# New durations in a list scheduler's model: an attention kernel with two feed-forward layers

## The chip, the cores and the metric

The kernel runs on one core of one Trainium2 chip. A core has five engines that each work through their own instructions in order: TensorE (PE, matrix products), VectorE (DVE), ScalarE (ACT), GpSimd (POOL) and SyncE (SP, which here issues all DMAs). They wait for one another by semaphores. The metric is device time in microseconds (us) of the whole kernel, the median of several runs; lower is better.

## The reference

```python
def _attn_ref(q, k, v, f):                     # (4, 8, 576, 64), f: (4, 8, 576)
    scores = scale * np.matmul(q, k.transpose(0, 1, 3, 2))
    cum = np.cumsum(np.log(np.clip(f, 0.0001, 1.0)), axis=-1)
    scores = np.where(causal, -1e9, scores + cum[..., :, None] - cum[..., None, :])
    return softmax(scores) @ v
def _moe_ref(x, w_in, w_out):                  # x: (2304, 512), w_in: (512, 2048)
    h = x @ w_in
    return np.maximum(0.01 * h, h) @ w_out
def _moe2_ref(x, w_in, w_out, g_ln):           # w_in: (512, 1024)
    h = x @ w_in
    solu = h * softmax(h)
    return (layer_norm(solu) * g_ln) @ w_out
```

The three run one after the other: causal attention with decay (4 batches, 8 heads, 576 positions), a feed-forward layer (FFN) on 2304 tokens with a hidden width of 2048, and a second layer with a width of 1024, whose activation is followed by a normalization.

## The kernel before

**Work and tiles.** Every fp32 product is made of three fp32r products of split operands: each operand is stored as a high part and the rest (`copy_f` makes the high part, `sub_f` the rest). Attention works on 16 pairs of heads (4 pairs for each batch). Of a pair, `prep_split` loads and splits q and k (`raw` to `kq`), `prep_v` scales and splits v, `scores` and `scores4` make the masked scores in PSUM tiles `ps_s`, `softmax` does maximum, exp (L647), sum, reciprocal and the split into f16 (`hl`), a DMA transposes `hl` to `pt`, `pv` multiplies by v into `ps_v`, and `evac` writes `xr` (L729 on ACT, L732 on DVE), which is spilled to DRAM as `xs_d`. The first four pairs are done in two passes, `(0, 1)` and `(2, 3, 4)` of their row blocks.

The FFN works on nine blocks of 256 tokens and 16 chunks of 128 hidden columns. `ffn_a` does chunks 0 to 8 (`FA`) while attention is still running, as far as batches are done: `load_x` brings x back as `xw` and splits it into `x`, `hidden` makes `ps_f<-x,wi` and its leaky ReLU `g` (L843 and L844 on ACT, L845 on DVE), and the output product is `ps_f<-g,wo`. Block 2 is the first that needs batch 1, block 4 the first that needs batch 2, block 6 the first that needs batch 3. When attention is finished, its SBUF and PSUM are handed to phase 2: `ffn_b` does chunks 9 to 15 (`wib`, `wob`) and `layer2` the second layer (`ph`, the normalization, a transposition through `tr`, and the output product). The weights are loaded and split by `weight` (`wst` or `raw`, an upper part `wk`, then the two parts).

**What sets the order.** Nothing above is emitted in the order in which it is written. `P.op` records each step as an `Op` with its engine (or several, for `flex` steps such as `copy_f` and `sub_f`), a duration in ns, a priority and the buffers that it writes and reads. `Plan.run` then walks through time: whenever an engine is free in its model, the ready step with the lowest priority number is emitted on it, a `flex` step only if `better_elsewhere` finds no engine on which it would end earlier. So the modelled durations decide two things: the order of each engine's instructions, and which engine does a `flex` step. On the chip each engine then runs its list in order and waits by semaphores. The model of before has three kinds of durations:

```python
def dve(n):                              # VectorE, n columns; act() and pool1() are alike
    return 1.042 * n + 70
def mmr(n):                              # a matmul of n columns
    return n / 2.4 + 2.5 if n > 255 else 80.0
```

a rule for the matmul clock, `pe_time`, which doubles a matmul's duration while PE was not busy enough in the windows before, and a single DMA queue with a rate (`nbytes / 360.0`).

## Time and profile before

| | us |
|---|---|
| median of 3 runs | 852.63 (852.53 to 854.60) |
| the profiled execution | 854.78 |
| its span, first to last instruction | 852.9 |
| PE busy | 787.6 |
| DVE, ACT, POOL busy | 495.8, 477.6, 338.6 |

A row of the profile that names `ps_f<-x,wi` is the instruction that writes tile ps_f and reads x and wi. Busy time is the union of an engine's instructions. An engine's idle time costs something only when the work behind it sets the end. L numbers are lines of the kernel of before; a helper's line stands for all that call it (L474 is every matmul, L428, L431 and L435 are `copy_f` on ACT, DVE and POOL, L443 is `sub_f`).

### The profile page before, as it was taken

How to read it: one execution, taken by the hardware profiler on the slowest of the kernel's cores; microseconds unless marked ns; L12 is line 12 of the kernel's file. 1: busy time of each engine (PE TensorE's matmuls, PEld its weight loads, DVE VectorE, ACT ScalarE, POOL GpSimd, SP SyncE). 2: the span in 40 equal slices, each digit the busy share in tenths (PEclk: the TensorE clock that was granted, in tenths of full speed). 3: DMA queues.
4: the chain of work that ended last, by engine and by line, in shares of the span. 5: the costliest groups of instructions: out<-in, count | busy, mean ns of one | idle time of the engine just before them, and what ended most of it. 6: DMA issues, size and time to landing. Idle time of an engine off the chain costs nothing.

```text
span 852.9 us, 15613 instructions
## 1 busy us (share of the span) xinstructions
PE 787.6 (92%) x5648; PEld 707.1 (83%) x5648; DVE 495.8 (58%) x1269; ACT 477.6 (56%) x1208; POOL 338.6 (40%) x402
## 2 busy tenths in 40 slices
PE   2567899997699999999999999999999999999997
PEld 2334599986699999999999988898889988998985
DVE  4787688787778768735544756334442444243641
ACT  3878788888888988845645533332333243324321
POOL 5566555474655484025121324321332133213321
PEclk9999989996799999999999999999999999999999
DMA  7899878899968997646555514231314131312113
GB/s 211 200 276 245 209 155 190 171 202 213 224 152 192 188 216 168 154 124 208 171 166 172 179 32 99 47 89 26 87 38 100 25 87 38 88 25 62 25 41 95
DMA packets 181958, 114.95 MB, mean 135 GB/s; under 512 B 147030, under 2 KB 163054, under 8 KB 181850
## 3 DMA queue, kind: packets, MB, share of 16 engines
q1 hardware_dynamic: 181882, 113.97, 55.5%
q8 instruction: 44, 0.72, 0.4%
q14 instruction: 32, 0.26, 0.1%
HBM read 64.32 MB, written 15.16 MB: 93 GB/s over the span
## 4 chain that ended last, share of the span: by engine, by line
PE 66%; ACT 7%; DMA 6%; DVE 5%; issue 3%; POOL 2%; SPq 0%; ACTq 0%; DVEq 0%; POOLq 0%
PE ps_f L474 41%; PE ph L474 11%; PE py L474 8%; PE ps_s L474 4%; PE ps_v L474 3%; DMA pt<-hl 3%; ACT hl L428 1%; ACT ps_s L647 1%; DMA xw<-xs_d 1%; DVE hl L439 1%; DMA tr<-hl 1%; ACT kq L428 1%; DMA raw<-wa 1%; ACT xr L729 1%; ACT g L843 1%
## 5 line engine op out<-in xcount | busy, mean ns | idle before, releaser
L474 PE MATMUL ps_f<-x,wi 128*128 128x256 f32 x972 | 131.4, 290 | 2.1 <-DVE g L845 2.1
L474 PEld LDWEIGHTS ps_f<-x,wi 128*128 128x128 f32 x972 | 124.9, 195 | 3.3 <-DVE g L845 2.9
L474 PE MATMUL ps_f<-g,wo 128*128 128x256 f32 x972 | 124.1, 283 | 0.0
L474 PEld LDWEIGHTS ps_f<-g,wo 128*128 128x128 f32 x972 | 119.3, 189 | 0.6 <-DVE g L845 0.2
L474 PE MATMUL ps_f<-x,wib 128*128 128x256 f32 x756 | 98.4, 281 | 0.7 <-DVE g L845 0.4
L474 PE MATMUL ph<-wi,g 128*128 128x512 f32 x408 | 98.3, 397 | 0.0
L843 ACT ACTIVATE g<-ps_f 128x256 fp32r<-128x256 f32 x144 | 55.1, 383 | 72.8 <-PE ps_f L474 70.9
L474 PEld LDWEIGHTS ps_f<-x,wib 128*128 128x128 f32 x756 | 92.8, 189 | 1.8 <-DVE g L845 1.7
L439 DVE SCALAR_TENSOR_TENSOR hl<-ps_s,st,hl 128x512 f16<-128x512 f32 (+4 forms) x160 | 82.4, 540 | 18.6 <-ACT hl L428 17.5
L474 PEld LDWEIGHTS ph<-wi,g 128*128 128x128 f32 x408 | 76.1, 189 | 17.5
L443 POOL TENSOR_TENSOR kq<-raw,kq 64x576 fp32r<-64x576 f32 (+2 forms) x49 | 74.0, 1510 | 36.6 <-ACT kq L428 34.2
L647 ACT ACTIVATE ps_s<-ps_s,st 128x512 f32<-128x512 f32 (+4 forms) x160 | 78.9, 493 | 15.7 <-DVE st L697 7.6
L474 PEld LDWEIGHTS <-VT 128*128 128x128 f16 x928 | 55.2, 108 | 37.2 <-issue 20.3
L474 PE MATMUL ps_f<-wo,x 128*128 128x512 f32 x348 | 84.0, 397 | 0.0
L845 DVE TENSOR_TENSOR g<-ps_f,g 128x256 fp32r<-128x256 f32 x144 | 60.3, 420 | 39.4 <-ACT ps_f L844 38.6
L474 PE MATMUL ps_v<-pt,VT 128*128 128x128 f16 (+1 forms) x928 | 63.2, 230 | 18.6 <-DVE xr L732 9.6
L474 PE MATMUL ps_s<-kq 128*128 128x512 f32 (+9 forms) x304 | 73.7, 365 | 6.8 <-DVE hl L439 6.7
L428 ACT ACTIVATE hl<-ps_s,st 128x512 f16<-128x512 f32 (+4 forms) x152 | 74.7, 529 | 9.1 <-DVE st L665 4.2
L474 PEld LDWEIGHTS ps_f<-wo,x 128*128 128x128 f32 x348 | 64.7, 189 | 15.1 <-ACT x L428 0.4
L474 PE MATMUL py<-g,wob 128*128 128x256 f32 x567 | 76.7, 280 | 0.0
L474 PEld LDWEIGHTS py<-g,wob 128*128 128x128 f32 x567 | 72.4, 188 | 1.9
L697 DVE CUSTOM_DVE_ANT_0 ps_s<-ps_s,mask 128x128 f32<-128x128 f32 (+3 forms) x128 | 62.3, 497 | 19.3 <-PE ps_s L474 17.1
(148 smaller groups left out, 1180.0 us busy)
## 6 DMA issues: line engine op xcount, KB each, us to landing
raw<-kq SPq DMA_DIRECT2D x24, 608.0 KB
wst<-wa SPq DMA_DIRECT2D x17, 512.0 KB
raw<-wa SPq DMA_DIRECT2D x15, 512.0 KB
xw<-xs_d SPq DMA_DIRECT2D x24, 256.0 KB
yp_d<-yo SPq DMA_DIRECT2D x36, 128.0 KB
yw<-yp_d SPq DMA_DIRECT2D x18, 256.0 KB
out<-ot SPq DMA_DIRECT2D x18, 256.0 KB
vr<-vt SPq DMA_DIRECT2D x13, 320.0 KB
```

What stands on the lines that cost most here:

```text
L428: nc.scalar.activation(o, i, CP, scale=1.0 if scale is None else scale)
L439: nc.vector.scalar_tensor_tensor(o, a, scale, b, op0=ALU.mult, op1=ALU.subtract)
L443: (nc.vector if eng == DVE else nc.gpsimd).tensor_tensor(o, a, b, op=ALU.subtract)
L474: nc.tensor.matmul(o, lhsT=l, rhs=r, start=start, stop=stop)
L647: P.op(ACT, act(W, 1, True) + 93, lambda view=view, j=j, k=k: nc.scalar.activation(view(), view(), AF.Exp, bias=sts.t[:, j:j + 1], scale=- ...
L697: P.op(DVE, dve(W) + 130, lambda i=i, j=j, view=view: nc.vector.tensor_tensor_reduce(view(), view(), mask[:, 384 - 128 * i:512], -0.125, 3 ...
L729: P.op(ACT, act(n, 1, True), lambda: nc.scalar.activation(xr.t[a:a + 64, dst0:dst0 + n], ps.t[b:b + 64, c0:c1], CP, scale=u.t[b:b + 64]), ...
L843: P.op(ACT, act(n, 0, True), lambda: nc.scalar.activation(g.t[:, 0, 0:n], h(), AF.Prelu, scale=WSC, alpha=0.01), eprio, w=[(g, 0)], r=[ps])
L845: P.op(DVE, dve(n) + 60, lambda: nc.vector.tensor_tensor(g.t[:, 1, 0:n], h(), g.t[:, 0, 0:n].bitcast(F32), op=ALU.subtract), eprio, w=[(g, ...
```

## The change

The change replaces numbers and one rule of the planner's model. `act`, `pool1`, `pool2`, `mmr`, `mmh` and the fixed parts of DVE steps become the durations of this kernel's own trace; a matmul of 256 columns goes from 109 to 119 ns, for instance. DMAs become slower in the model (`nbytes / 320.0`; a transposition takes 1.6 ns for each column of its source in the DMA queue and not 0.875). The clock rule `pe_time` is dropped. A new flag `port` marks DVE steps whose operands all lie in SBUF; `beside` stretches such a step to 1/0.58 of its length as long as the model has POOL busy. The steps themselves, buffers, priorities, weights and all other constants stay.

```diff
+LOCK = 0.58
...
-        def pe_time(d, t, heat):
...
+        def beside(d, t):
+
+            r = max(free_at["POOL"] - t, 0.0)
+            return d / LOCK if d <= LOCK * r else r + d - LOCK * r
...
                     hold = o.dur
-                    if e == "PE":
-                        hold = pe_time(hold, now, o.heat)
+                    if e == "DVE" and o.port:
+                        hold = beside(hold, now)
...
+def dvep(n):
+    return 1.05 * n + 125
...
 def act(n, extra=0, psum=False):
-    return 0.833 * n + (52 if psum else 95) + 93 * extra
+    return 0.83 * n + (150 if psum else 125) + 118 * extra
...
 def mmr(n):
-    return n / 2.4 + 2.5 if n > 255 else 80.0
+    return n * 0.4545 + 3.0 if n > 255 else 116.0
...
     def copy_f(o, i, n, prio, engs=(ACT, DVE, POOL), scale=None, psum=False, **kw):
         p = 0 if scale is None else 1
-        d = {ACT: act(n, p, psum), DVE: (dve(n) if psum else dve2(n)) + 60 * p, POOL: pool1(n) + 84 * p}
+        d = {ACT: act(n, 0, psum), DVE: dvep(n) if psum else dve2(n) + 30 * p, POOL: pool1(n) + 84 * p}
...
-        return flex(engs, [d[e] for e in engs], lambda e: queue[e].dma_start(dst(), src()), prio, dma=nbytes / 360.0, **kw)
+        return flex(engs, [d[e] for e in engs], lambda e: queue[e].dma_start(dst(), src()), prio, dma=nbytes / 320.0, **kw)
...
-        return P.op(SP, max(350.0 + 0.875 * n, 1175.0), lambda: nc.sync.dma_start_transpose(out=dst(), in_=src()), prio, dma=0.875 * n, **kw)
+        return P.op(SP, max(350.0 + 0.875 * n, 1175.0), lambda: nc.sync.dma_start_transpose(out=dst(), in_=src()), prio, dma=1.6 * n, **kw)
```

What comes of it in the order of the instructions, at three places.

On ACT, at the head of the program, where the first weights are split and the first softmax begins; before:

```order
L428 ACTIVATE wi_64<-wst_151 128x512
L428 ACTIVATE wk_83<-wst_152 128x512
L647 ACTIVATE ps_s_163,st_120<-ps_s_163,st_120 128x128
L609 ACTIVATE VT_106,va_136<-vr_105 128x640
L647 ACTIVATE ps_s_163,st_120<-ps_s_163,st_120 128x256
L609 ACTIVATE VT_107,va_137<-vre_156 128x640
```

and after (the lines stand 13 lower in the changed kernel, so L647 is L634):

```order
L415 ACTIVATE wi_64<-wst_151 128x512
L634 ACTIVATE ps_s_163,st_120<-ps_s_163,st_120 128x128
L634 ACTIVATE ps_s_163,st_120<-ps_s_163,st_120 128x256
L634 ACTIVATE ps_s_164,st_121<-ps_s_164,st_121 128x128
L646 ACTIVATE st_120<-st_120 128x2
L634 ACTIVATE ps_s_165,st_122<-ps_s_165,st_122 128x128
```

The weight copy to wk_83 has moved to POOL, and the sums over v (L609) stand behind more exps.

On PE, where FFN block 2 begins (the first row with x and wi) among the scores of a pair; before:

```order
L474 MATMUL ps_s_163<-kq_0_143 128x64
L474 MATMUL ps_s_163<-kq_1_144 128x64
L474 MATMUL ps_f_157<-x_810,wi_63 128x256 x3
L474 MATMUL ps_f_157<-x_811,wi_63 128x256 x3
L474 MATMUL ps_f_157<-x_812,wi_63 128x256 x3
L474 MATMUL ps_f_157<-x_813,wi_63 128x256 x3
```

and after:

```order
L461 MATMUL ps_v_167<-pt_132,VT_106 128x128
L461 MATMUL ps_s_166<-kq_0_143 128x128
L461 MATMUL ps_s_166<-kq_1_144 128x128
L461 MATMUL ps_f_158<-x_782,wi_63 128x256 x3
L461 MATMUL ps_f_158<-x_783,wi_63 128x256 x3
L461 MATMUL ps_f_158<-x_784,wi_63 128x256 x3
L461 MATMUL ps_f_158<-x_785,wi_63 128x256 x3
```

A further group of PV products (20 matmuls into ps_v) and four score products now stand ahead of block 2.

On PE, behind the last PV product of attention; before:

```order
L474 MATMUL ps_v_167<-pt_131,VT_109 128x128
L474 MATMUL ps_f_158<-g_824,wo_78 128x256 x3
L474 MATMUL ps_f_158<-g_825,wo_79 128x256 x3
L474 MATMUL ps_f_158<-g_826,wo_80 128x256 x3
L474 MATMUL ps_f_158<-g_827,wo_72 128x256 x3
```

and after:

```order
L461 MATMUL ps_v_167<-pt_131,VT_109 128x128
L461 MATMUL ps_f_158<-x_786,wi_69 128x256 x3
L461 MATMUL ps_f_158<-x_787,wi_69 128x256 x3
L461 MATMUL ps_f_158<-x_788,wi_69 128x256 x3
L461 MATMUL ps_f_158<-x_789,wi_69 128x256 x3
```

Attention now ends while block 5 is still in its hidden product; three more chunks of it and the whole of its output product follow.

## Rows read from the trace of the kernel before

**Rows 1.** The page: busy time of the engines, PE and its clock in 40 slices

```profile
PE 787.6 (92%) x5648; PEld 707.1 (83%) x5648; DVE 495.8 (58%) x1269; ACT 477.6 (56%) x1208; POOL 338.6 (40%) x402
...
PE   2567899997699999999999999999999999999997
...
PEclk9999989996799999999999999999999999999999
```

**Rows 2.** Busy time (instructions) by stretch, us: PE, PEld, DVE, ACT, POOL, clock, DMA

```profile
0.00:100.00 100.00, 62.54 (x240) 37.61 (x241) 69.45 (x200) 67.87 (x163) 59.42 (x68) 1.00 0.90 230
100.00:180.00 80.00, 75.24 (x675) 70.80 (x674) 64.99 (x202) 67.32 (x192) 43.91 (x44) 0.96 0.81 175
180.00:240.00 60.00, 46.03 (x345) 41.45 (x344) 45.38 (x150) 50.40 (x138) 37.66 (x37) 0.77 0.93 213
240.00:365.00 125.00, 123.74 (x1202) 119.99 (x1201) 95.77 (x316) 108.13 (x310) 58.10 (x61) 1.00 0.83 176
365.00:416.00 51.00, 49.53 (x421) 49.07 (x420) 22.62 (x37) 24.35 (x61) 18.79 (x22) 1.00 0.60 182
416.00:814.00 398.00, 397.08 (x2638) 362.41 (x2637) 184.10 (x350) 150.53 (x334) 112.98 (x160) 1.00 0.31 79
814.00:853.00 39.00, 33.44 (x141) 25.74 (x139) 13.51 (x20) 8.97 (x15) 7.75 (x13) 0.98 0.24 61
```

**Rows 3.** Timeline of the head: start, length in us, instruction, idle time before it

```profile
17.46 0.14 DVE L697 DVE_READ_ACCUMULATOR2_ANT st<- 128x1 f32 x1
...
18.66 0.78 ACT L428 ACTIVATE wk<-wst 128x512 f16<-128x512 bf16 x1 [6.82 <-DMA wst<-wa]
19.31 0.31 ACT L647 ACTIVATE ps_s<-ps_s,st 128x128 f32<-128x128 f32 x1
```

**Rows 4.** Groups by line and shape on ACT: count, busy us, mean ns, idle before

```profile
L428 ACT ACTIVATE kq<-raw 128x1216 fp32r<-128x1216 f32 x12 | 14.6, 1217 | 2.5 <-DMA raw<-kq 1.3 <-PE ps_s L474 1.2
...
L428 ACT ACTIVATE x<-xw 128x256 fp32r<-128x256 f32 x39 | 14.4, 411 | 4.5 <-DMA xw<-xs_d 4.3
...
L428 ACT ACTIVATE kq<-kq 64x640 fp32r<-64x640 f32 x12 | 8.8, 731 | 0.1
...
L428 ACT ACTIVATE VT<-vre,vs 128x640 f16<-128x640 f32 x2 | 1.6, 811 | 0.0
```

**Rows 5.** Timeline around the start of FFN block 2

```profile
213.92 0.33 SPq L465 DMA_DIRECT2D xs_d<-xr  x1
...
218.56 2.11 SPq L465 DMA_DIRECT2D xw<-xs_d  x4
...
223.95 3.00 PE L474 MATMUL ps_f<-x,wi 128*128 128x256 f32 x12
```

**Rows 6.** Pieces of the chain that ended last: start, us, what

```profile
209.97 2.16 PE ps_v L474 x20
...
352.53 0.36 PE ps_s L474 x4
...
354.40 1.13 PE ps_v L474 x20
...
416.78 52.51 PE ps_f L474 x432
```

**Rows 7.** Timeline: a DVE and a POOL instruction side by side

```profile
110.00 1.54 POOL L443 TENSOR_TENSOR kq<-raw,kq 64x640 fp32r<-64x640 f32 x1
110.05 2.11 DVE L443 TENSOR_TENSOR kq<-raw,kq 64x576 fp32r<-64x576 f32 x1
```

**Rows 8.** DVE's longest waits from 240 to 365 us: total, times, longest

```profile
DVE ps_s L697 <- PE ps_s L474: 6.8, 9, 1.5
DVE hl L439 <- ACT hl L428: 6.3, 13, 1.1
```

**Rows 9.** Timeline of phase 2: a block's last output products, splits of y, ph

```profile
487.08 0.52 PE L474 MATMUL ps_f<-g,wob 128*128 128x256 f32 x3
...
489.41 2.02 POOL L443 TENSOR_TENSOR g<-yo,g 128x256 fp32r<-128x256 f32 x2
...
491.69 3.67 PE L474 MATMUL ph<-wi,g 128*128 128x512 f32 x15
```

More of the change, by code (lines that the diff above doesn't have):

```diff
@@ L92 @@
 class Op:
-    __slots__ = ("eng", "dur", "emit", "bufs", "prio", "npred", "succ", "seq", "taken", "dma", "weight", "heat")
+    __slots__ = ("eng", "dur", "emit", "bufs", "prio", "npred", "succ", "seq", "taken", "dma", "weight", "heat", "port")
 WEIGHT = {"DVE": 4.25}
@@ L171, in run @@
         left = len(self.ops)
-        warm, win, busy = False, 0, 0.0
         def push(t, kind, x):
@@ L218, in bequeath @@
                     self.tags[nm].free.append(view)
-        def pe_time(d, t, heat):
-            nonlocal warm, win, busy
-            k = int(t // WINDOW)
-            while win < k:
-                u = busy / WINDOW
-                warm = u > 0.8 or (warm and u > 0.38)
-                busy, win = 0.0, win + 1
-            end = t
-            while d > 1e-6:
-                edge = (win + 1) * WINDOW
-                f = 1.0 if warm else 2.0
-                step = min(d * f, edge - end)
-                d -= step / f
-                end += step
-                busy += step * heat
-                if end >= edge - 1e-6:
-                    u = busy / WINDOW
-                    warm = u > 0.8 or (warm and u > 0.38)
-                    busy, win = 0.0, win + 1
-            return end - t
+        def beside(d, t):
+            r = max(free_at["POOL"] - t, 0.0)
+            return d / LOCK if d <= LOCK * r else r + d - LOCK * r
         for o in self.ops:
@@ L453, in copy_f, with sub_f @@
         p = 0 if scale is None else 1
-        d = {ACT: act(n, p, psum), DVE: (dve(n) if psum else dve2(n)) + 60 * p, POOL: pool1(n) + 84 * p}
-        return flex(engs, [d[e] for e in engs], lambda e: copy_on(e, o(), i(), scale and scale()), prio, **kw)
-    def sub_f(o, a, b, n, prio, engs=(DVE, POOL), scale=None, **kw):
-        d = {DVE: dve(n) + (60 if scale else 0), POOL: pool2(n) + (pool1(n) + 40 if scale else 0)}
-        return flex(engs, [d[e] for e in engs], lambda e: sub_on(e, o(), a(), b(), scale and scale()), prio, **kw)
+        d = {ACT: act(n, 0, psum), DVE: dvep(n) if psum else dve2(n) + 30 * p, POOL: pool1(n) + 84 * p}
+        return flex(engs, [d[e] for e in engs], lambda e: copy_on(e, o(), i(), scale and scale()), prio, port=not psum, **kw)
+    def sub_f(o, a, b, n, prio, engs=(DVE, POOL), scale=None, psum=False, **kw):
+        d = {DVE: dvep(n) if psum else dve(n) + (60 if scale else 0), POOL: pool2(n) + (pool1(n) + 40 if scale else 0)}
+        return flex(engs, [d[e] for e in engs], lambda e: sub_on(e, o(), a(), b(), scale and scale()), prio, port=not psum, **kw)
     queue = {SP: nc.sync, ACT: nc.scalar, POOL: nc.gpsimd}
@@ L672, in softmax @@
                 sub_f(lambda lo=lo, w=w: hl.t[:, lo:lo + w], lambda so=so, w=w, view=view: view()[:, so:so + w],
-                      lambda ho=ho, w=w: hl.t[:, ho:ho + w], w, prio, engs=(DVE,), scale=rs,
+                      lambda ho=ho, w=w: hl.t[:, ho:ho + w], w, prio, engs=(DVE,), scale=rs, psum=True,
                       w=[(hl, lo)], r=[ps, (sts, 4), (hl, ho)])
@@ L731, in evac @@
             w=[(xr, (hd, dst0))], r=[ps, u])
-        P.op(DVE, dve(n) + 60, lambda: nc.vector.scalar_tensor_tensor(
+        P.op(DVE, 0.97 * n + 240, lambda: nc.vector.scalar_tensor_tensor(
             xr.t[a:a + 64, dst0:dst0 + n], ps.t[a:a + 64, c0:c1], u.t[a:a + 64],
@@ L801, in weight @@
         copy_f(up, top, 512, prio, engs=T_ENGS, scale=lambda: 0.5, w=[k], r=[s])
-        P.op(DVE, dve(512), lambda: nc.vector.scalar_tensor_tensor(
-            low(), low(), 13, k.t, op0=ALU.logical_shift_right, op1=ALU.bitwise_or), prio, rw=[s], r=[k])
+        P.op(DVE, dve(512) + 40, lambda: nc.vector.scalar_tensor_tensor(
+            low(), low(), 13, k.t, op0=ALU.logical_shift_right, op1=ALU.bitwise_or), prio, rw=[s], r=[k], port=True)
         copy_f(lambda: dst.t[:, 0], kf, 512, prio, scale=scale, w=[(dst, 0)], r=[s])
@@ L843, in hidden @@
         P.op(ACT, act(n, 0, True), lambda: nc.scalar.activation(g.t[:, 0, 0:n], h(), AF.Prelu, scale=WSC, alpha=0.01), eprio, w=[(g, 0)], r=[ps])
-        P.op(ACT, act(n, 0, True), lambda: nc.scalar.activation(h(), h(), AF.Prelu, scale=WSC, alpha=0.01), eprio, rw=[ps])
-        P.op(DVE, dve(n) + 60, lambda: nc.vector.tensor_tensor(
+        P.op(ACT, act(n, 0, True) - 90, lambda: nc.scalar.activation(h(), h(), AF.Prelu, scale=WSC, alpha=0.01), eprio, rw=[ps])
+        P.op(DVE, dve(n) + 10, lambda: nc.vector.tensor_tensor(
             g.t[:, 1, 0:n], h(), g.t[:, 0, 0:n].bitcast(F32), op=ALU.subtract), eprio, w=[(g, 1)], r=[ps, (g, 0)])
```

18 lines of the change are left out of this document (9 added, 9 removed).

## The prediction

> **What bounds the kernel now.** I read the page first, then the busy time of the engines in seven stretches, then the waits and the timeline of the stretches in which TensorE (PE) stands idle. The page says that PE is busy for 92% of the span, far more than the others, and its row of slices shows where it is not: in the first quarter, in two slices near 200 us, and in the last slice [rows 1]. The stretches put numbers on it [rows 2]. From 416 to 814 us PE is busy for 397.08 of 398 us: there the FFN runs with hardly a gap and no order can gain anything. From 240 to 365 us it is busy for 123.74 of 125. What is idle lies elsewhere: 37.5 us before 100 us, 4.8 us from 100 to 180, 14.0 us from 180 to 240, 1.5 us around the switch from attention to FFN (365 to 416), and 5.6 us in the tail after 814. In the stretch from 180 to 240 the granted clock is also only 0.77, so the matmuls there run in part at the lower level: twenty attention matmuls took 2.16 us at 210 us and 1.13 us at 354 us [rows 6].
>
> So the end is "the time at which PE becomes full" plus "the PE work left at that time" plus small change. PE becomes full when FFN block 2 can start. That block needs the attention of all eight heads of batch 1, its spill to DRAM, the reload and the split of x; until then PE has only scores and PV, and the chain of exp, reciprocal, copy and transpose sets the pace. In that time ScalarE (ACT) is the fullest of the other engines: 67.32 of 80 us and then 50.40 of 60 us [rows 2], against 64.99 and 45.38 for VectorE (DVE). The spill of the last head pair of batch 1 is issued at 213.92 us, x comes back by DMA issues at 218.56, and the matmuls of block 2 run from 223.95 us on [rows 5].
>
> **The change part by part.** It removes and adds no arithmetic. It changes the numbers that the planner believes, so each engine gets another order, and the instructions that may run on several engines are dealt out otherwise. PE has 5648 matmuls before and after. I went through both orders and priced what stands ahead of the same place in each by the mean durations of before.
>
> *The head.* Before, ACT's eighth row is a weight copy (wk from wst_152) that waits 6.82 us for its load; the first exp stands behind it and starts at 19.31 us, though the row maximum it needs is read out by 17.60 us (17.46 + 0.14) [rows 3]. After, the copy is on GpSimd (POOL) and the exp comes directly after the two weight splits, at 17.6 us if nothing else holds it: 1.7 us earlier. Bounds: 0, if the loads set the pace anyway (the DMA share of the first 100 us is 0.90 [rows 2]), and 1.7. I take 1.7, since ACT carries the whole softmax that follows: **-1.7 us**.
>
> *ACT and DVE up to block 2.* Up to the first evacuation of block 2, ACT has 360 rows instead of 366: five copies kq to kq fewer at 731 ns (-3.7), five x copies fewer at 411 ns (-2.1), but two raw to kq more at 1217 ns (+2.4), three V scalings more at 811 ns (+2.4) [rows 4], and a few smaller ones, among them a further piece of softmax: in sum +0.8 us. DVE has 13 rows more there, +2.7 us in sum. Both do that extra work for attention that has moved ahead of block 2 (next part). Since ACT is the fuller one, I take **+0.8 us**, and 2.7 us as the bound if DVE sets the time.
>
> *PE up to block 2.* Before, 502 PV matmuls and 192 score matmuls stand ahead of block 2; after, 522 and 196. Twenty PV matmuls cost 1.13 us at full clock and four score matmuls 0.36 us [rows 6]. They run in time that is idle and are then missing from the full stretch: **-1.5 us**, with bounds 0 and -2.5 (their price at the low clock).
>
> *Attention against FFN up to 373 us.* After, 1152 of the 1944 matmuls of the first FFN half stand ahead of the last PV, before 1200. These 48, at 52.51 us for 432 [rows 6], are 5.8 us of FFN that moves behind attention. Up to ACT's last evacuation its work falls by 5.9 us: seven kq to kq copies fewer (-5.1), three x copies fewer (-1.2), three FFN evacuation pairs fewer (-2.3), against three V scalings (+2.4) and others [rows 4]. So attention can end some 5 us earlier, and the FFN that is left is as much more: no gain by itself. But where block 6 needs the last batch, its first matmul now has 15.3 us of other matmuls behind the last PV instead of 11.4. PE's idle time there is 1.5 us [rows 2]; I take a third of it back, **-0.5 us**, with bounds 0 and -1.5.
>
> *Phase 2 and tail.* The loop over hidden chunks, final product and layer 2 keeps its form; PE was full there, so it can only lose. The tightest place: behind the last W_out matmuls of a block the split of y must be ready for the next ph. Before, at least 36 matmuls of other work stand between (4.2 us), after, 24 (2.8 us) in three of nine blocks. In the trace the last of these matmuls end at 487.60 us, ph starts at 491.69 us, and the last POOL split ends at 491.43 us, 3.8 us behind [rows 9]. ph needs the first quarter of y at its start and the last only half way through, so I take 0; if it waited for everything, 1.0 us three times, 3.0 us. From a ph to its output product there are at least 18.2 us after and 18.3 us before: no change. In the tail the same rows stand in the same order on PE and DVE, and one split copy moves from ACT to POOL: **0**, bounds -0.6 and +0.6.
>
> *Sum.* -1.7 + 0.8 - 1.5 - 0.5 = -2.9 us. The profiled execution took 854.78 us (span 852.93), which makes 851.9. The median of the runs shown, 852.63 us, lies 2.15 us under the profiled one, so the forecast for the median is 849.7 us.
>
> **What speaks against the model.** It stretches a DVE instruction beside GpSimd to 1/0.58 of its length. At 110.05 us a DVE subtraction of 576 columns began 0.05 us behind a POOL subtraction that ran to 111.54, and took 2.11 us; it ended 0.62 us after POOL's [rows 7]. 0.62 us is about its own time (the model has 670 ns), so it stood still. With 0.58 the planner expects 1.16 us and believes DVE free 0.95 us too early. The Trainium skill says the same (SBUF — State Buffer, "Who interferes with whom"): a DVE instruction with two SBUF inputs beside a GpSimd instruction that reads SBUF does not share, the second one to issue is blocked until the first ends. By that page a plan that counts on sharing comes out late on DVE.
>
> **The rivals.**
> 1. *ScalarE sets the pace all through attention, and a better plan takes away its waits as well.* From 15 us to the last evacuation its load falls by 5.9 us, and all of that comes off the end, with the 1.7 us of the head: 852.6 - 7.6 = 845.0. For it: ACT is busy for 108.13 of 125 us from 240 to 365. Against it: PE is full there too [rows 2], so a faster ACT finds PE taken.
> 2. *The order does not matter at this scale.* The loads and PE's own work set the times; the head's gain is lost in the first 100 us with a DMA share of 0.90, and only PE's 1.5 us or less stay: 851.5 to 852.6.
> 3. *VectorE becomes the bound, and it ends slower.* Between block 2 and block 5 DVE must do more for the same FFN progress: at the 46th FFN evacuation +8.1 us of work stand ahead, and PE has some 3.6 us of attention more behind it. DVE's waits from 240 to 365 us are long (its two longest kinds 6.8 and 6.3 us [rows 8]), and so far the extra work fits in. If it does not, because blocked instructions as at 110 us fall on it, DVE runs 8.1 us late with 3.6 us less left on PE: +4.5, and 857.1. It decides from the point at which DVE's extra work and blocking exceed its 29 us of idle time in that stretch (125 - 95.77).
> 4. *An engine queue in order.* The priorities were fitted to the old model. If one late row, say a ph behind a late split (3.0 us as above) or a transpose queued on SyncE behind another's wait, holds PE where it was full: 855 to 857.
>
> **How the numbers follow.** A measurement tells a difference over about 0.3% (2.6 us, so 850.1 and 855.2). Forecast 0.40 (849.7; of that 0.25 faster and 0.15 within 0.3%), rival 1 0.17 (845.0), rival 2 0.13 (within), rival 3 0.20 and rival 4 0.10 (slower). Faster 0.42, same 0.28, slower 0.30. The forecast's own range is 846 to 853. For 8 in 10 I go to 841 on the low side (rival 1 with the waits on weight loads gone as well) and to 862 on the high side (rivals 3 and 4 together, 852.6 + 4.5 + 4.4).
>
> **What would show it.** Head: the first exp near 17.6 us. Block 2: first matmul of its hidden layer earlier than 223.95 us, PE idle time from 180 to 240 us under 14 us. Attention: last PV some 5 us earlier. Phase 2: PE idle time still near 1 us in 398 us, and no wait in front of ph. If DVE waits almost nowhere from 240 to 365 us and PE waits for it, rival 3 is right; if the first exp is early and block 2 is not, rival 2. I am wrong altogether if PE shows new idle time behind 240 us, where it was full, since every us of it is a us of the end.

## The result and the profile after

The changed kernel is slower. Its median is 864.31 us (862.55 to 866.26) against 853.62 us for the kernel before on the same chip: a ratio of 1.0122, 95% interval 1.0087 to 1.0157. The forecast was 849.7 us. One run of before among those of the experiments took 886.28 us, at a granted clock of 0.858, and is left out of all ratios.

The profiled execution of after took 862.55 us (span 860.5), 7.6 us more in the span than before's (852.9). The rest of the difference between the medians is that before's profiled run lay 1.2 us above the median of its runs, and after's 1.8 us below.

The page of after: busy time of the engines, then PE and its clock in 40 slices (beside [rows 1]).

```profile
PE 788.6 (92%) x5648; PEld 707.7 (82%) x5648; DVE 507.3 (59%) x1286; ACT 467.1 (54%) x1188; POOL 338.4 (39%) x404
...
PE   2467899996699999999999999999999999999997
...
PEclk9999999997599999999999999999999999999999
```

The stretches of after; columns as in [rows 2], after the width: busy us (instructions) of PE, PEld, DVE, ACT and POOL, granted clock, DMA share, GB/s.

```profile
0.00:100.00 100.00, 55.31 (x204) 33.26 (x205) 63.66 (x193) 62.11 (x150) 50.74 (x62) 1.00 0.78 205
100.00:180.00 80.00, 78.62 (x674) 72.44 (x672) 63.87 (x208) 71.67 (x198) 47.23 (x45) 1.00 0.92 206
180.00:240.00 60.00, 45.56 (x352) 40.37 (x351) 44.63 (x147) 47.16 (x123) 36.20 (x39) 0.72 0.86 192
240.00:365.00 125.00, 123.19 (x1186) 118.89 (x1186) 104.56 (x323) 106.98 (x314) 63.45 (x68) 1.00 0.86 185
365.00:416.00 51.00, 50.26 (x433) 49.67 (x430) 22.76 (x43) 27.07 (x67) 20.47 (x22) 1.00 0.59 183
416.00:814.00 398.00, 394.30 (x2638) 360.53 (x2637) 191.00 (x352) 142.58 (x322) 106.34 (x151) 1.00 0.29 78
```

PE has the same 5648 matmuls, busy for 1.0 us more. So 6.6 of the 7.6 us are idle time of PE, and the width less the first number of each row says where, beside [rows 2]:

| stretch, us | idle before | idle after | difference |
|---|---|---|---|
| 0 to 100 | 37.5 | 44.7 | +7.2 |
| 100 to 180 | 4.8 | 1.4 | -3.4 |
| 180 to 240 | 14.0 | 14.4 | +0.5 |
| 240 to 365 | 1.3 | 1.8 | +0.5 |
| 365 to 416 | 1.5 | 0.7 | -0.7 |
| 416 to the end | 6.4 | 8.8 | +2.4 |

The differences are taken before rounding. The large entry is the head. PE lost 7.2 us there, and from 100 to 180 us it idled 3.4 us less; phase 2 adds 2.4. Attention itself got nothing back: the 120th PV matmul in PE's order starts at 99.8 us (before 91.2), the 501st, one of the last ahead of block 2, at 228.5 us (before 220.5), so it is 8.6 us and then still 8.0 us late. This is PE's timeline in the head of after (start, length, instruction, idle time before it and what ended that):

```profile
37.31 0.85 PE L461 MATMUL ps_v<-pt,VT 128*128 128x128 f16 x6
40.20 0.82 PE L461 MATMUL ps_v<-pt,VT 128*128 128x128 f16 x6 [2.04 <-DVE xr L719]
43.05 0.48 PE L461 MATMUL ps_f<-ident,va 128*128 128x128 f32 x1 [2.04 <-ACT VT L596]
43.33 0.86 PE L461 MATMUL ps_v<-pt,VT 128*128 128x128 f16 x6
49.56 0.82 PE L461 MATMUL ps_v<-pt,VT 128*128 128x128 f16 x6 [5.37 <-POOL VT L430]
50.17 2.02 PE L461 MATMUL ps_s<-qb 66*128 66x512 f32 x2
```

and this is before, at the same place:

```profile
39.49 0.80 PE L474 MATMUL ps_v<-pt,VT 128*128 128x128 f16 x6 [0.41 <-DVE xr L732]
40.05 0.46 PE L474 MATMUL ps_f<-ident,va 128*128 128x128 f32 x1
40.30 3.29 PE L474 MATMUL ps_s<-qb 66*128 66x512 f32 x4
```

Before, the first score products over a whole batch (ps_s from qb) stand behind 18 PV matmuls and start at 40.30 us. After, they stand behind 30. PE takes its rows in order; it waits 5.37 us for a V tile that GpSimd has not finished, with the scores behind it, and these start at 50.17 us. What hangs on the scores then has less to do: from 40 to 60 us DVE is busy for 11.37 us instead of 16.94, PE for 11.41 instead of 13.82.

In phase 2 a wait is there that before does not have. PE's waits from 590 to 830 us in after (total, times, longest); before has none in that stretch:

```profile
PE ps_f L461 <- DVE g L832: 3.2, 6, 0.8
PE py L461 <- DVE g L832: 0.3, 1, 0.3
```

One of them on the timeline of after:

```profile
601.12 0.87 DVE L960 TENSOR_SCALAR raw<-raw,s 128x1024 f32<-128x1024 f32 x1 [1.09 <-POOL s L957]
...
601.92 0.41 DVE L832 TENSOR_TENSOR g<-ps_f,g 128x256 fp32r<-128x256 f32 x1
...
602.38 4.01 PE L461 MATMUL ps_f<-wo,x 128*128 128x512 f32 x16 [0.48 <-DVE g L832]
```

VectorE's row g, which frees a PSUM buffer, stands behind a normalisation that waits 1.09 us for GpSimd; the output product that needs the buffer waits 0.48 us. Six output products wait so, 0.5 us each on average.

Block 2, the place on which the forecast rested, started later instead of earlier. The places of [rows 5] in after:

```profile
217.73 0.34 SPq L452 DMA_DIRECT2D xs_d<-xr  x1
221.21 2.13 SPq L452 DMA_DIRECT2D xw<-xs_d  x4
...
236.43 2.38 PE L461 MATMUL ps_f<-x,wi 128*128 128x256 f32 x12
```

236.43 us, not before 223.95. Behind that start PE has, in before and then in after, this left to do:

```profile
223.95:853.00 629.05, 617.01 (x4472) 569.64 (x4472) 327.34 (x750) 305.91 (x757) 207.69 (x265) 0.99 0.45 109
```

```profile
236.43:861.00 624.57, 612.70 (x4448) 565.22 (x4448) 336.85 (x744) 288.84 (x724) 206.34 (x262) 1.00 0.43 108
```

Block 2 starts 12.5 us later, 4.3 us less work is left, and PE idles 0.6 us less behind it up to the end of the span (11.4 instead of 12.0): that is the 7.6 us. The last PV matmul of attention ended at 372.3 us (before 372.8), with 48 FFN matmuls more still to do.

### The profile page after: what moved, and what is told of

The parts are those of the page before. It is cut to its first block, busy times and chain, and to the rows that moved or that the text cites. A ratio compares the mean times of both kernels' runs of the same rounds, so it can differ in the third digit from the quotient of the medians.

```text
span 860.5 us, 15621 instructions
## 1 busy us (share of the span) xinstructions
PE 788.6 (92%) x5648; PEld 707.7 (82%) x5648; DVE 507.3 (59%) x1286; ACT 467.1 (54%) x1188; POOL 338.4 (39%) x404
## 4 chain that ended last, share of the span: by engine, by line
PE 66%; DVE 11%; ACT 6%; issue 4%; DMA 3%; POOL 2%; SPq 0%; DVEq 0%; POOLq 0%; ACTq 0%
PE ps_f L461 39%; PE ph L461 11%; PE ps_s L461 7%; PE py L461 4%; PE ps_v L461 4%; DVE hl L426 2%; ACT ps_s L634 1%; DMA raw<-w2o 1%; ACT hl L415 1%; DVE raw L943 1%; DVE g L832 1%; DVE s L935 1%; DMA tr<-hl 1%; DVE s L948 1%; ACT raw L937 1%
## 5 line engine op out<-in xcount | busy, mean ns | idle before, releaser
L461 PE MATMUL ps_f<-x,wi 128*128 128x256 f32 x972 | 127.7, 287 | 1.1 <-DVE g L832 1.1
L461 PEld LDWEIGHTS ps_f<-x,wi 128*128 128x128 f32 x972 | 122.2, 192 | 1.7 <-DVE g L832 1.5
L634 ACT ACTIVATE ps_s<-ps_s,st 128x512 f32<-128x512 f32 (+4 forms) x160 | 78.9, 493 | 24.8 <-DVE st L684 16.8
L426 DVE SCALAR_TENSOR_TENSOR hl<-ps_s,st,hl 128x512 f16<-128x512 f32 (+4 forms) x160 | 82.0, 539 | 16.4 <-ACT hl L415 14.9
L415 ACT ACTIVATE hl<-ps_s,st 128x384 f16<-128x384 f32 (+4 forms) x150 | 73.9, 532 | 11.5 <-issue 2.2
L461 PEld LDWEIGHTS ps_f<-wo,x 128*128 128x128 f32 x348 | 64.5, 188 | 18.2 <-DVE g L832 3.5
L461 PE MATMUL ps_v<-pt,VT 128*128 128x128 f16 (+1 forms) x928 | 64.7, 232 | 15.8 <-DVE xr L719 6.9
```

The source lines that it names most:

```text
L415: nc.scalar.activation(o, i, CP, scale=1.0 if scale is None else scale)
L426: nc.vector.scalar_tensor_tensor(o, a, scale, b, op0=ALU.mult, op1=ALU.subtract)
L461: nc.tensor.matmul(o, lhsT=l, rhs=r, start=start, stop=stop)
L634: P.op(ACT, act(W, 1, True), lambda view=view, j=j, k=k: nc.scalar.activation(view(), view(), AF.Exp, bias=sts.t[:, j:j + 1], scale=-1.0, ...
```

## Experiments

All of them leave the computation whole, and change only the order of work (delay40 repeats some of it). For most of them the changed kernel got a switch for each part of the change, apart for the operations of attention and first FFN half (first number of a pair) and of phase 2 (second):

```diff
+NEW, DMA, CLOCK, PORT = (1, 1), (1, 1), (0, 0), (1, 1)
+def pick(new, old, table=None):
+    return new if (table or NEW)[NOW[0]] else old
...
 def dvep(n):
-    return 1.05 * n + 125
+    return pick(1.05 * n + 125, dve(n))
...
-                    if e == "DVE" and o.port:
+                    if e == "PE":
+                        hold = pe_time(hold, now, o.heat) if CLOCK[o.part] else hold
+                    elif e == "DVE" and o.port and PORT[o.part]:
```

The line as it stands stands for after, and (0, 0), (0, 0), (1, 1), (0, 0) for before. This table holds all kernels: PV matmuls ahead of the first full scores in PE's order, PE's idle time by stretch of the profiled run (width less busy time), the median, and its ratio to the runs of before on the same chip with the 95% interval. The kernels ran on several chips, so the ratios are to be compared, not the medians; the idle times are those of one execution each.

| kernel | PV ahead | 0-100 | 100-240 | 240-416 | from 416 | median us | ratio |
|---|---|---|---|---|---|---|---|
| before | 18 | 37.5 | 18.7 | 2.7 | 6.4 | 853.6 | 1 |
| after | 30 | 44.7 | 15.8 | 2.6 | 8.8 | 864.3 | 1.0122 (1.0087 to 1.0157) |
| stage1_new | 30 | 44.3 | 17.6 | 4.6 | 9.8 | 867.1 | 1.0163 (1.0134 to 1.0192) |
| stage2_new | 18 | 37.1 | 15.1 | 1.7 | 9.5 | 853.7 | 1.0016 (0.9997 to 1.0036) |
| noport | 30 | 50.4 | 18.9 | 4.3 | 14.8 | 876.9 | 1.0270 (1.0230 to 1.0310) |
| clockback | 12 | 39.8 | 15.7 | 3.4 | 8.6 | 854.3 | 1.0011 (0.9991 to 1.0032) |
| clk_head | 12 | 37.5 | 15.3 | 2.3 | 9.7 | 856.2 | 1.0017 (0.9987 to 1.0047) |
| clk_gap | 30 | 45.4 | 21.6 | 3.0 | 9.5 | 866.1 | 1.0151 (1.0119 to 1.0183) |
| headfix | 30 | 46.6 | 16.7 | 4.4 | 8.8 | 864.3 | 1.0122 (1.0082 to 1.0161) |
| yfirst | 30 | 44.4 | 18.2 | 2.3 | 10.1 | 864.7 | 1.0140 (1.0089 to 1.0191) |
| headfix2 | 18 | 44.3 | 15.8 | 2.1 | 8.6 | 863.0 | 1.0107 (1.0069 to 1.0144) |
| headclk_old2 | 12 | 37.4 | 16.5 | 5.0 | 9.5 | 860.4 | 1.0071 (1.0047 to 1.0095) |
| olddma | 12 | 35.8 | 11.5 | 9.1 | 9.1 | 855.2 | 1.0009 (0.9975 to 1.0044) |
| onlydma | 36 | 48.4 | 15.7 | 0.6 | 8.5 | 859.4 | 1.0071 (1.0047 to 1.0094) |
| delay40 | 18 | 39.0 | 14.2 | 5.3 | 6.3 | 868.5 | 1.0153 (1.0108 to 1.0199) |
| noclk_only | 24 | 39.3 | 19.0 | 7.0 | 6.2 | 860.4 | 1.0064 (1.0026 to 1.0102) |
| olddma_old2 | 12 | 37.7 | 13.8 | 9.4 | 9.7 | 858.3 | 1.0030 (0.9996 to 1.0063) |
| onlydur | 12 | 35.9 | 15.8 | 9.7 | 11.6 | 869.1 | 1.0160 (1.0116 to 1.0203) |
| act101 | 12 | 37.0 | 16.4 | 2.0 | 6.7 | 850.8 | 0.9956 (0.9930 to 0.9982) |
| pe101 | 18 | 38.4 | 19.7 | 3.9 | 8.9 | 856.4 | 1.0042 (1.0015 to 1.0068) |

### Which stage, which rule

The first theory was that after loses in the gap before block 2 and in phase 2. Four kernels tell stages and rules apart.

**stage1_new**: `(1, 0), (1, 0), (0, 1), (1, 0)`.

> The new numbers (durations, DMA, no clock rule, the stretch) for the operations of attention and the first FFN part alone; phase 2 is planned with the old ones. Up to 365 us the order is after's; in phase 2 the output product W (24 matmuls, ps_f<-wo,x) stands right behind a hidden product in 3 places, as in before, and not in 10 as in after. Theory: after loses in two separate places, some 4 to 6 us around the gap before block 2 (200 to 240 us) and some 3 to 5 in phase 2; this kernel has the first alone: 858 us (856.5 to 860). Rival 'the head': the late qb load carries all of it: 863 to 865. Rival 'phase 2 carries it all': 853 to 855. Rival 'any new plan costs 1%': 860 to 866, and what the two halves cost does not add up to after.

**stage2_new**: `(0, 1), (0, 1), (1, 0), (0, 1)`.

> The new numbers for the operations of phase 2 alone; attention and the first FFN part are planned with the old ones, so up to block 5 the order is before's (502 PV matmuls ahead of block 2), and W stands right behind a hidden product in 10 places, as in after. Theory: the phase 2 loss alone, 0.48 us for each W that waits for VectorE's g: 857 us (855.5 to 859). Rival 'the head': 853 to 855. Rival 'any new plan costs 1%': 860 to 866.

**noport**: `(1, 1), (1, 1), (0, 0), (0, 0)`.

> After without the stretch of VectorE beside GpSimd in the model; all its other numbers. In the order: 522 PV matmuls ahead of block 2 as in after (before 502), W right behind a hidden product in 10 places as in after, 1092 FFN matmuls ahead of the last PV matmul (after 1152, before 1200). Theory (the places, not the rule, cost the time): 860 to 867. Rival 'the stretch is the culprit': back at 852 to 856.

**clockback**: `(1, 1), (1, 1), (1, 1), (1, 1)`.

> After with the model's clock rule (PE at half speed after idle stretches) put back; all its other numbers. In the order: 522 PV matmuls ahead of block 2, W right behind a hidden product in 10 places, 1152 FFN matmuls ahead of the last PV matmul, all as in after. Theory: 860 to 866. Rival 'the dropped clock rule is the culprit': back at 852 to 856.

The new numbers in phase 2 alone cost nothing that can be told from 0 (853.7; the interval allows up to 0.4%), although this kernel's idle time from 416 us on is 3.1 us above before's: its first stage idled 5 us less in its profile. Up to 332 us PE has before's order there, so most of these 5 us is what two executions of one order differ by. The new numbers in the first stage alone cost as much as the whole change, or more (867.1, above what was expected; its interval and that of after overlap). The stretch of VectorE is not the culprit: without it the plan is worse still, 876.9, more than was expected. And the theory's places fall with clockback: it has after's 522 PV matmuls ahead of block 2 and after's ten output products right behind a hidden product, and is as fast as before. What it does not have is after's head.

### Head or gap

**clk_head** and **clk_gap** apply the clock rule only before or only behind 100 us of the planner's time (`FROM, TILL` in ns):

```diff
-                        hold = pe_time(hold, now, o.heat) if CLOCK[o.part] else hold
+                        hold = pe_time(hold, now, o.heat) if CLOCK[o.part] or FROM <= now < TILL else hold
```

> After, with the clock rule in the model's first 100 us alone (clockback, with the rule everywhere, took 854.3 us; after 864.3). In the order: the loads of the full score operands on SP's queue stand as in clockback (the decay rows of pair 0 at row 37, pair 2 at row 56; in after 42 and 64), 502 PV matmuls ahead of block 2 as in before, W right behind a hidden product in 10 places. Theory 'head': the rule was worth its 10 us by the order up to 100 us, where after lost 5.1 us of PE work and the first full scores came 10 us late: 853 to 857. Theory 'gap': the head is made good by 200 us, the loss is in the gap before block 2: this order has before's row there too, so 855 to 859. Rival 'chance' (any plan falls anywhere in 853 to 877): no number.

> After, with the clock rule from the model's 100 us on alone. In the order: the head is after's, word for word up to 100 us (decay rows of pair 0 at SP row 42, pair 2 at 64); 502 PV matmuls ahead of block 2, as in before. Theory 'gap': 855 to 858, the head's loss is made good by 200 us. Theory 'head': 861 to 866.

Columns as above; clk_head first, then clk_gap:

```profile
0.00:100.00 100.00, 62.48 (x230) 37.43 (x230) 71.21 (x207) 67.96 (x162) 61.65 (x71) 1.00 0.88 228
100.00:240.00 140.00, 124.66 (x1067) 116.54 (x1068) 115.80 (x370) 114.97 (x326) 83.75 (x80) 0.89 0.89 200
```

```profile
0.00:100.00 100.00, 54.58 (x189) 32.52 (x190) 62.77 (x192) 61.19 (x148) 49.82 (x61) 1.00 0.77 204
100.00:240.00 140.00, 118.43 (x1005) 108.02 (x1005) 109.78 (x350) 114.65 (x316) 79.80 (x75) 0.91 0.93 200
```

The rule in the head alone brings the time back to before's (856.2, not told from 1), and in the rest alone it brings nothing (866.1). PE does 7.9 us more work in the head with clk_head's order, and ends 11.7 us earlier in the span. The PV matmuls say the same: clk_head's 120th and 501st start at 92.3 and 220.9 us, close to before's, clk_gap's at 100.8 and 229.7 us, as late as after's or later. Both plans have 502 PV matmuls ahead of block 2, and PE has clockback's order in clk_head up to 195 us and after's order in clk_gap up to 117 us.

What the rule says of the head is right. The 1.00 in the rows of the first 100 us is no measurement: the trace's first record of the clock is at 100.9 us in before and at 115.2 us in after, and time without a record counts as 1.00. The matmuls themselves run at the pace of the lower level: in after, PV matmuls of 128 columns start 107 ns apart at 43 us, as at 213 us, where the granted clock is 0.50 (1.2 GHz), and 56 ns apart at 195 us, where it is 1.00 (2.4 GHz). The new model without the rule prices one at 56 ns (`mmh(128)`), half of what it takes in the head. That a planner which prices PE too fast puts the PV products ahead of the scores, since it believes them done early, is a reading that no run shows by itself.

### Time lost in the head

Two edits move rows of after by hand. **headfix** moves three loads on SP's queue, and **headfix2** also brings pair 0's first three full-score products forward with what hangs on them:

```diff
 def mend(line):
+    sp = [o for o in line if o.eng == "SP"]
+    q = [o for o in sp if any(b.tag.name == "qb" for b in o.bufs)]
+    ahead(line, q[2] if len(q[2].pred) > len(q[1].pred) else q[1], sp[A0])
+    ahead(line, q[5], sp[A1])
+    ahead(line, q[4], sp[A1])
...
+A0, A1 = 42, 61
...
+    early = {scores[0]: pvs[3], scores[1]: pvs[4], scores[2]: pvs[4]}
```

The second part, from `early` on, is headfix2's alone.

> After with three loads on SP's queue moved by hand, nothing else: the decay rows of pair 0 (qb<-df_d) from row 42 to 36, the two loads of pair 2 from 64, 65 to 59, 60; PE's order is after's. Theory 'head by SP's order': the first full scores (50.17 us in after, 40.30 in before) come 5 to 8 us earlier, and of after's loss some 3 to 6 us go: 858 to 861. Theory 'gap': PE catches up by 200 us anyway: 862.5 to 865.

> After, with the head's order mended by hand and nothing else touched: pair 0's first three full-score products stand behind 18 and 24 PV matmuls on PE (before 18 and 24; after 30, 36 and 36, the last ones waiting 5.4 us for GpSimd's VT), what hangs on them on VectorE, ScalarE, GpSimd and SP's queue comes forward with them, and the decay rows of pair 0 go from row 42 to 36. Theory 'head, in order on PE': the first full scores start near 40 to 44 us (after 50.17, before 40.30), PE's idle time to 100 us falls from 30.8 us to some 24 to 27, and the end comes 3 to 6 us earlier: 858 to 861. Rival 'made good by 200 us' or 'elsewhere': 863 to 866, as headfix, which moved the loads alone.

headfix changed nothing (864.3): PE's order stayed, PE stands in front of the PV rows whatever SP loads, and the first full scores start at 52.9 us, not earlier than in after. headfix2 gave 863.0, which its interval does not tell from after; the theory's 858 to 861 is missed. On its timeline the scores did come forward, to 43.72 us, and the wait went to the next row in order:

```profile
43.72 2.02 PE L545 MATMUL ps_s<-qb 66*128 66x512 f32 x2
...
59.85 0.47 PE L545 MATMUL ps_f<-ident,va 128*128 128x128 f32 x1 [4.58 <-ACT VT L680]
```

Up to 100 us PE idled 44.3 us, as in after (44.7; the 30.8 of the expectation is not this count), and the 120th PV matmul starts at 99.4 us, as late as in after. So moving these three products forward does not mend the head; which rows make it, on which engines, stays open.

That left open whether a loss in the head reaches the end at all. **delay40** asks this alone, in before:

```diff
+    qb = [o for o in line if o.eng == "PE" and any(b.tag.name == "qb" for b in o.bufs)]
+    if qb:
+        once = qb[0].emit
+        qb[0].emit = lambda: [once() for _ in range(TIMES)]
...
+TIMES = 9
```

> Before, with pair 0's first full-score matmul (128x512, 1.02 us, at 40.3 us) run nine times in place of once into the same place; nothing else. It takes 8.2 us of TensorE's time at 41 us and holds up the attention behind it, as after's head does (8.1 us more of idle time up to 100 us). Theory 'the head's loss is carried': 100 to 180 us gives back the 3.4 us of idle time that after got back there, the rest stays: 857 to 862. Rival 'made good by 200 us': 853 to 855.5.

The edit met more than the text says: 18 matmuls of 66x512 ran in place of 2 (the others of the group below are two of 66x384 behind them), so 16 too many at 0.85 us start to start, or 13.7 us (16.95 here, 3.29 in before).

```profile
41.79 16.95 PE L541 MATMUL ps_s<-qb 66*128 66x512 f32 x20
```

The end came 14.7 us later in the span, and the median 13.9 us. The 120th PV matmul starts 15.0 us later than in before (106.2 us), the 501st 16.0 us later (236.5 us). So what PE and attention lose at 41 us is carried to the end in full. PE's idle time adds up to 64.7 us against before's 65.3: from 180 to 240 us it fell from 14.0 to 9.0 us, but the work has shifted there, and from 240 to 416 us it rose from 2.7 to 5.3. That is the direct answer: a delay at this place finds no slack behind it.

### Which numbers make the head

**olddma**: `(1, 1), (0, 0), (0, 0), (1, 1)`; **onlydma**: `(0, 0), (1, 1), (1, 1), (0, 0)`; **noclk_only**: `(0, 0), (0, 0), (0, 0), (0, 0)`; **onlydur**: `(1, 1), (0, 0), (1, 1), (0, 0)`.

> After with the old two DMA numbers (360 bytes/ns and 0.875 for a transposed column in place of 320 and 1.6), no clock rule, all other numbers new. In the order: first full scores behind 12 PV matmuls, decay rows of pair 0 at SP row 33; 502 PV ahead of block 2; no W right behind a hidden product. Theory 'head': 853 to 857, since a plan whose full scores come early is as good as before, whichever number made them early. Rival 'the clock rule itself': 861 to 868.

> Before with the two new DMA numbers alone; clock rule and old durations. In the order: first full scores behind 36 PV matmuls, decay rows of pair 0 at SP row 49, later than in after; 522 PV ahead of block 2. Theory 'head': 861 to 870 although the clock rule is there. Rival 'the clock rule itself': 852 to 856.

> Before with the clock rule taken out of the model and nothing else. In the order: the first full scores behind 24 PV matmuls (before 18, after 30), the decay rows of pair 0 at SP row 46 (before 35, after 42), W right behind a hidden product in 3 places as in before. Theory 'head, by its order': between before and after, 856 to 862. Rival 'the rule is worth its 10 us by itself': 862 to 867. Rival 'the rule is nothing without the new DMA numbers': 852 to 855.

> Before with the new durations of the operations alone; clock rule, old DMA numbers and no stretch. In the order: first full scores behind 12 PV matmuls, decay rows of pair 0 at SP row 35; W right behind a hidden product in 3 places; 1077 FFN matmuls ahead of the last PV, the fewest of all plans (before 1200, after 1152). Theory 'head': 852 to 857. Rival 'what counts is how much of the FFN part stands ahead of the last PV': 862 or more.

After with the two DMA numbers put back is as good as before (855.2), with no clock rule at all; and before with the new DMA numbers alone loses 0.7% though it keeps the rule (expected 861 to 870, measured 859.4; its 48.4 us of idle time up to 100 us is the most but for noport). Dropping the rule alone costs 0.6%. So either change alone costs about half of what the whole change costs, and in the whole change either of them put back undoes it. Both push the whole-batch scores back, the DMA numbers far more: with them alone the decay rows of pair 0 are issued at 55.80 us and the first full scores start at 59.7 us (before 34.87 and 40.3), with the rule dropped alone at 38.87 and 43.5 us. noclk_only idles only 1.8 us more than before up to 100 us and 4.3 us more from 240 to 416 us, so its loss is not shown to be in the head.

onlydur is the miss that counts. Its head is early and idles the least but one (35.9 us), and it is among the slowest, 869.1 (863.64 to 869.64; the profiled execution is the fastest). What it gained it lost behind 240 us. PE's waits from 365 to 500 us, olddma first, then onlydur:

```profile
PE ps_f L496 <- DVE g L867: 7.1, 7, 1.6
```

```profile
PE ps_f L496 <- DVE g L867: 5.8, 4, 2.2
PE ps_f L496 <- DVE yo L943: 1.8, 1, 1.8
```

An early head lets attention end early (357.8 us in olddma, 356.3 in onlydur, 372.8 in before), but there is then nothing but FFN left for PE, and it waits for VectorE's g from block to block. olddma's idle time from 240 to 416 us is 9.1 us, before's 2.7. These waits are much alike in the two kernels, so they do not say why onlydur is slower than olddma; that stays open. So the head accounts for after, but a good head is not enough for a fast plan.

### Phase 2, and a faster version

**yfirst** puts a Y product between the hidden product and six of the ten output products:

```diff
+        for a, b in zip(pe, pe[1:]):
+            if b.emit.__name__ == "pe2" and "hidden" in a.emit.__qualname__:
+                y = next((o for o in pe[pe.index(b):] if "ffn_b" in o.emit.__qualname__), None)
+                if y is not None and line.index(y) - line.index(b) < 200:
+                    ahead(line, y, b)
```

> After with six of phase 2's output products W put behind the next Y by hand on PE, so that a Y stands between the hidden product and W as in before; nothing else. Theory: each of these W no longer waits 0.48 us for VectorE's g, and the 3.5 to 4.3 us that the orders with 10 such places lost between 600 and 814 us (after, stage2_new, clockback; stage1_new lost nothing there) shrink by 2 to 3: 861 to 862.5. Rival: the wait moves to the next hidden product, 864.

The waits of yfirst from 590 to 830 us:

```profile
PE py L536 <- DVE g L907: 3.5, 6, 1.6
PE ps_f L536 <- DVE g L907: 0.8, 1, 0.8
```

The rival is right: the wait went from the output product to the next Y, which needs the same g. By these rows the wait hangs on VectorE, where g stands behind a row that waits, and not on PE's order; no run moved that row.

**headclk_old2** (clk_head with the old numbers in phase 2) and **olddma_old2** (olddma with them) tried to join a good head with before's phase 2.

> clk_head (new numbers, clock rule in the first 100 us) with the old numbers for the operations of phase 2. In the order: first full scores behind 12 PV matmuls, W right behind a hidden product in 3 places. Theory: the head costs nothing and phase 2's 2.7 us of PE idle time (from 2.0 in before to 4.7 in after) go: 851 to 854. Rival: both losses are chance of the plan, 856 or more.

> olddma (new durations and stretch, no clock rule, old DMA numbers) with the old numbers for the operations of phase 2. olddma's attention ended at 357.8 us with 474.9 us of TensorE work left (before: 372.8 and 469.1), but then TensorE idled 18.4 us (before 11.1), 4.5 of it waiting for VectorE's g between 390 and 424 us. Theory: the early head is worth up to 9 us, and phase 2 in its old order idles less: 847 to 852, faster than both kernels. Rival: the end of the first FFN part gives the gain back whatever phase 2 does: 853 to 857.

Both missed, olddma_old2 its rival's range too. From 600 us on the waits are gone, as expected, but new ones came between 416 and 500 us, where the two plans meet: headclk_old2 still idles 9.5 us from 416 us on, olddma_old2 9.7. The pieces of the two plans did not add up here.

That raised the rival that any new plan costs time, since offsets and priorities of the planner were set with the old one. **act101** and **pe101** make the smallest new plans, before with every duration of one engine 1% longer:

```diff
+        if isinstance(eng, tuple):
+            dur = tuple(d * 1.01 if e == 'ACT' else d for e, d in zip(eng, dur))
+        elif eng == 'ACT':
+            dur = dur * 1.01
```

> Before with every ScalarE duration in the model 1% longer; nothing else. In the order: first full scores behind 12 PV matmuls (before 18), 522 PV ahead of block 2 (before 502), 1176 FFN matmuls ahead of the last PV (before 1200). Theory 'the new numbers make the bad head': a 1% change leaves the time at before's, 851 to 856.5. Rival 'before is a picked plan, any other costs some per cent': 857 to 866.

> Before with every TensorE duration in the model 1% longer; nothing else. In the order: the head as in before (18 PV matmuls ahead of the first full scores), 502 PV ahead of block 2, 1188 FFN matmuls ahead of the last PV. Theory 'the new numbers': 851 to 856.5. Rival 'any other plan costs': 857 to 866.

act101 is 0.4% faster than before, 850.8 us, and so faster than both kernels; pe101 is 0.4% slower. The stretches of act101:

```profile
0.00:100.00 100.00, 63.04 (x244) 38.88 (x245) 71.02 (x204) 66.84 (x162) 63.00 (x75) 1.00 0.88 225
100.00:240.00 140.00, 123.63 (x1065) 115.88 (x1063) 113.56 (x370) 116.97 (x331) 88.31 (x87) 0.85 0.86 202
240.00:416.00 176.00, 173.96 (x1597) 169.40 (x1596) 126.60 (x350) 131.60 (x365) 69.31 (x72) 1.00 0.73 178
```

Its idle time adds up to 62.0 us against 65.3, 2.4 of the difference between 100 and 240 us; it too has 522 PV matmuls ahead of block 2. Nobody chose this plan: in these two draws a 1% change of numbers moved the time by 0.4%, one each way. Each plan here must be held against at least that scatter. After's 1.2% is three times as much, and every plan with 30 or more PV matmuls ahead of the full scores is slow (seven of seven, 0.7 to 2.7%), though five of them share after's head. Fewer do not make a plan fast: headfix2, headclk_old2, noclk_only and onlydur, with 12 to 24, are 0.6 to 1.6% slow. So the head as the place of after's loss rests on clk_head against clk_gap and on delay40, more than on that count.

## Why the prediction was wrong

**What bounds the kernel.** The formula, the time at which PE becomes full plus the work left, held: 12.5 us later, with 4.3 us less work left and 0.6 us less idle time. The reading of the first 240 us did not: the idle time there was taken as room in which PE work is free, and the lower level of the clock was seen only from 180 to 240 us, though PE's matmuls run at its pace in the head too. delay40 shows that the room is not free; 13.7 us put into it came out as 14.7 us at the end.

**The head, -1.7 us.** The step was right for what it looked at: the first exp starts at 17.74 us (17.6 forecast), and the first evacuation of PV on ACT 0.6 us earlier than before (35.16 instead of 35.79). But the head was followed only to 20 us. From 36 to 60 us PE's own order changed, and by 100 us PE had idled 7.2 us more. This is the term that failed, by 9 us: what the new order does to PE itself in the head was put at nothing without a reason, and the dropped clock rule stands in no term. In its place the runs show a head in which PE waits 5.37 us for a V tile with the full scores behind it, attention 8.0 us late at the end of batch 1, and the loss gone when the clock rule is put back for the head alone (clk_head). It could have been read: both orders and the mean durations were at hand, and the wait of the PV rows for V shows as soon as PE's rows up to 60 us are laid side by side. The orders were compared by what stands ahead of block 2, where the head's changes cancel.

**ACT and DVE up to block 2, +0.8 us.** ACT's load was right and did not decide. ACT's busy time up to 365 us fell by 5.8 us ([rows 2] against the rows above), the 5.9 that was forecast; the end of attention did not move by it. Rival 1 built on that load falls with it.

**PE up to block 2, -1.5 us.** The 20 PV and four score matmuls are ahead of block 2, but it began 12.5 us later, and PE idled 14.4 us from 180 to 240 instead of less than 14.0. They need be no loss: clockback and act101 have the same 522 PV matmuls there and are as fast as before or faster.

**Attention against FFN, 0.** The 5.8 us of FFN are indeed left over, but the last PV matmul came at 372.3 us and not 5 us earlier. The lag of 8 us at block 2 is used up by then, with those 48 FFN matmuls left for later.

**Block 6, -0.5 us.** Idle time from 365 to 416 us fell by 0.7 us. That fits, but is no proof: in stage1_new, which shares after's order up to 328 us, it is 1.8 us, more than before's 1.5.

**Phase 2 and tail, 0.** Wrong by 2.4 us of idle time. The tightest place was looked for before ph, and ph does not wait. The waits are for VectorE's g, six of some 0.5 us, since its row stands behind a normalisation that waits for GpSimd. The order of VectorE in phase 2 was not compared. The bounds of the term, -0.6 and +0.6, missed that; the 3.0 us named for ph would have covered it, with another cause. Of the end these 2.4 us explain little: stage2_new has 3.1 us and is not told from before.

**What speaks against the model, and rival 3.** VectorE did get fuller, 104.56 us of 125 from 240 to 365 us instead of 95.77, and its subtractions of x took 827 ns instead of 661, before first:

```profile
L443 DVE TENSOR_TENSOR x<-xw,x 128x256 fp32r<-128x256 f32 x26 | 16.6, 661 | 1.1 <-ACT x L428 0.7 <-POOL x L435 0.3
...
L430 DVE TENSOR_TENSOR x<-xw,x 128x256 fp32r<-128x256 f32 x28 | 22.2, 827 | 1.8 <-ACT x L415 1.4 <-POOL x L422 0.3
```

But PE was busy for 123.19 of these 125 us, so VectorE did not become the bound. The stretch in the model did no harm that shows: noport, without it, is slower by another 1.5%, with the worst head of all (50.4 us idle).

**Rival 4** is what happened in kind, one row in order in front of another's work. It was sought where PE is full, and priced at 855 to 857, 2.4 to 4.4 us; it sat where PE is idle anyway, and cost 7.2 us of idle time there. Rival 2's sign came too, an early first exp and a late block 2, but its 851.5 to 852.6 us did not. So did the sign for being wrong altogether, idle time behind 240 us, with 2.2 us; it is not where the time went. The range, 841 to 862, ended 2.3 us short of the time.

**Left open.** Which rows make the head late is not shown, since headfix2 did not mend it. Why act101 is faster is known only as idle time by stretch. Why g is late between 390 and 500 us in plans with an early head was seen and not tried.

## What to carry to other kernels

Idle time of the engine that bounds the whole is not free room when it stands in a chain: what is lost in front of it is carried to the end, so the order of the bounding engine has to be laid beside the old one row by row where it idles, not where it is full. Ask of a number that a change takes away whether it was right: the dropped clock rule was, in the head, and the 1.00 in the profile's rows there is a missing record, which the start-to-start times of like matmuls give away. What one number costs hangs on the others (the new DMA numbers cost 0.7% alone, and stand in clockback, which is as fast as before); put such numbers in one at a time and time each plan. Measure first how far a 1% change of the planner's numbers moves the time (0.4% in two draws here), since a gain below that can be a draw of the plan.

## What the runs showed of the hardware

PE runs at the lower level in two places above all. The first is the head, where PE idles much (44.7 of the first 100 us in after), the page shows 1.00 without a record behind it, and PV matmuls of 128 columns start 107 ns apart. The second lies near 200 us: in every kernel the granted clock is 0.97 to 1.00 from 240 to 365 us, and between 0.72 and 0.89 from 180 to 240 us. In after it falls to 0.50 at 203.9 us and rises at 238.1 us. Before it fell, PE was busy for 10.71 of 14 us (190 to 204 us), before it rose for 9.73 of 13 us (225 to 238 us). The place moves with the work: in delay40, where attention runs 15 to 16 us late, it falls at 215.9 us, in before at 199.9 us. A group of 20 PV matmuls took 1.29 us at 195.53 us and 2.36 us at 213.08 us in after, 17.6 us apart:

```profile
195.53 1.29 PE L461 MATMUL ps_v<-pt,VT 128*128 128x128 f16 x20
...
213.08 2.36 PE L461 MATMUL ps_v<-pt,VT 128*128 128x128 f16 x20
```

The time of one kernel scatters more than its first runs showed: before ran from 848.9 to 861.4 us over 90 runs on five chips, each at a granted clock of 0.974 to 0.986. Its three runs at the start lay within 2.1 us. With some ten runs on each side a difference of 0.3% is at the edge of what can be told.
